# Transposes by DMA, a new order of TensorE's work, and a new division of the exponentials in a two-layer attention and gMLP kernel

## Chip, cores and metric

One core of a Trainium2 chip. The metric is the device time of one execution in microseconds (us). The record marks a run as slow when it is over 1.5% above the fastest of the same kernel. Each kernel's ratio is taken against runs of the kernel before on the same chip in the same rounds. Differences between two experiments are differences of medians, in part from other rounds and chips; the kernel before had medians of 1791.0 to 1793.1 us in all of them.

## The reference

Two layers, each an attention (32 query heads of 16, one key/value head) and a gated MLP with a spatial matrix `w_sp` of 2048 x 2048. S = 2048, D = 512.

```python
x = x + A(layernorm(x)); x = x + B(layernorm(x))      # twice, the same weights

def A(x):                                             # H = 32, Dh = 16
    q = (x @ wq).reshape(B, S, H, Dh).transpose(0, 2, 1, 3); k = x @ wk; v = x @ wv
    p = softmax(einsum('bhqd,bkd->bhqk', q, k) * Dh ** -0.5)
    return einsum('bhqk,bkd->bhqd', p, v).transpose(0, 2, 1, 3).reshape(B, S, H * Dh) @ wo

def B(x):
    z = gelu(x @ w_in); z1 = z[..., :896]; z2 = layernorm(z[..., 896:])
    g = einsum('ts,bsf->btf', w_sp, z2) + b_sp[None, :, None]
    return (z1 * g) @ w_out
```

The cost sits in the exponentials: 2 x 32 x 2048 x 2048 of them, in 4096 score blocks of 128 x 512 (in the kernel before ScalarE is busy with its part of them for 1474.0 of 1791.3 us).

## The kernel before

The program is scheduled in Python at build time: every operation is a task with a modelled cost, an event loop picks what each engine does next, and the order of each engine's instructions is then fixed.

```python
SHARE = 0.24; POOL_MAX = 4500; ACT_LOW = 1500; PV_MAX = 2      # (cut)
PASSES = ((0, 8), (8, 12), (12, 14), (14, 16))   # row tiles of each spatial pass
TERMS = ((0, 0.324...), (43, 0.253...), (85, 0.200...))        # three ramps: offset, weight

def do_exp(...):            # ScalarE: one or two score blocks at a time, PSUM -> slots of Pb
    e.activation(self.Pb[...], self.ps32[...], ACTF.Exp, scale=ESCALE)

def dve_block(...):         # or: three ramps in the bits of bf16 numbers
    # the first by VectorE from the score bank in PSUM (now and then another one too)
    e.tensor_scalar(self.Pi[:, sl[v].i, :], self.ps32[:, bank.i, :], EBIAS + lo, lo, op0=ALU.add, op1=ALU.max)
    # the others by GpSimd from the first one's slot in SBUF
    e.tensor_scalar(self.Pi[:, sl[v].i, :], self.Pi[:, sl[0].i, :], lo, 1.0, op0=ALU.add, op1=ALU.mult)

def step_pe(self):          # TensorE: scores, then value matmuls, then anything that is ready
    ...

def wsp_build(self):        # w_sp: 16 loads of 512 KB, 256 transposes on TensorE, copies, stores to HBM
    ...
```

The program's names in the profile: `ps_all` is the tile in PSUM that takes TensorE's results, in banks that must come free again; `Pb` is the tile in SBUF that holds the exponentials, in slots (`Pi` is the same tile read as int16). A block that goes to ScalarE takes one slot of `Pb` and one value matmul; an approximated block takes three of each.

The softmax here doesn't subtract the row's maximum and nothing guards it: scores larger than these inputs give would overflow.

## Time and profile before

| | before |
|---|---|
| time (median of 4) | 1792.14 us (1789.02 to 1794.14) |
| ScalarE busy / idle | 1579.6 / 211.7 us of a 1791.3 us span |
| exponentials' blocks on ScalarE / approximated | 3115 / 981 |

The prediction shows the totals, the slices, five stretches and the main groups. A group's line reads: line of the kernel, engine, operation, tile written <- tiles read, shapes, count | busy us, mean ns of one | idle us before it, and who ended that. A line of waits reads: who <- for whom: us in total, times, longest us. Two more readings matter later: the chain that ended last (the page's part 4, shares of the span by engine), and GpSimd's ramp by itself (shortest, median and longest in ns). The chain of the kernel before:

```profile
ACT 47%; PE 34%; POOL 8%; DVE 5%; issue 4%; DMA 1%; SPq 1%; DVEq 0%; ACTq 0%
```

Then the ramps that GpSimd makes, by line:

```profile
L1256 POOL TENSOR_SCALAR Pb<-Pb x1929: 619/620/742, 41.5 to 1719.4; 128x512 int16<-128x512 int16 x193
```

GpSimd's ramp takes 620 ns nearly always: only 7 of the 1929 take over 630. ScalarE leads the chain with 47%.

### The profile page before, as it was taken

The page shows a single profiled execution, that of the slowest core. Times are in us where ns is not written, and L with a number is a line of the kernel's source. Part 1 is how long each engine was busy: PE and PEld are TensorE (multiplying, and loading weights), DVE is VectorE, ACT ScalarE, POOL GpSimd, SP SyncE. Part 2 cuts the span into 40 slices and gives each one's busy share as a digit, 9 for nine tenths or more (in the row PEclk, how much of TensorE's full clock was granted, in tenths as well). Part 3 has the DMA queues.
Part 4 walks back from the last instruction along what each step waited for, and adds up shares of the span by engine and source line. Part 5 has one row for each costly group of instructions (what it writes and reads, how often), then busy time and mean ns, then how long its engine had stood idle before and what let it go on. Part 6 is the DMA issues. An engine that isn't in the chain of part 4 may idle for free.

```text
span 1791.3 us, 37444 instructions
## 1 busy us (share of the span) xinstructions
PE 1598.1 (89%) x14507; PEld 552.8 (31%) x14638; DVE 1116.0 (62%) x1894; ACT 1579.6 (88%) x2240; POOL 1341.0 (75%) x2262
## 2 busy tenths in 40 slices
PE   3999988888999999998999888887899999999998
PEld 2433322222322223233654222322232222233245
DVE  4777654455655575776876645555475566657766
ACT  2999999999899999997547999999999999999950
POOL 3788878788888887886346888788887888878830
PEclk9999999899999999999999999999999999999999
DMA  6015600000000000000000000000000000000001
GB/s 198 10 43 133 168 14 1 2 1 1 1 28 28 28 1 28 7 13 13 25 31 13 1 1 1 1 1 1 1 1 1 28 27 28 2 30 7 13 25 48
DMA packets 61662, 45.04 MB, mean 25 GB/s; under 512 B 35504, under 2 KB 58928, under 8 KB 61488
## 3 DMA queue, kind: packets, MB, share of 16 engines
q1 hardware_dynamic: 61488, 42.64, 8.2%
q8 instruction: 119, 1.95, 0.5%
q14 instruction: 55, 0.45, 0.1%
HBM read 32.15 MB, written 10.49 MB: 24 GB/s over the span
## 4 chain that ended last, share of the span: by engine, by line
ACT 47%; PE 34%; POOL 8%; DVE 5%; issue 4%; DMA 1%; SPq 1%; DVEq 0%; ACTq 0%
ACT Pb L1295 46%; PE ps_all L1167 8%; PE ps_all L1347 8%; POOL Pb L1256 6%; PE ps_all L997 5%; PE ps_all L897 3%; PE ps_all L939 3%; DVE Pb L1241 2%; PE ps_all L1051 2%; PE ps_all L703 1%; PE ps_all L1029 1%; ACT L1482 1%; POOL xn L568 1%; SPq L479 1%; PE ps_all L1027 1%
## 5 line engine op out<-in xcount | busy, mean ns | idle before, releaser
L1295 ACT ACTIVATE Pb<-ps_all 128x1024 bf16<-128x1024 f32 (+1 forms) x2053 | 1474.0, 961 | 48.5 <-PE ps_all L1167 40.2
L1256 POOL TENSOR_SCALAR Pb<-Pb 128x512 int16<-128x512 int16 x1929 | 1196.3, 620 | 277.0 <-DVE Pb L1241 135.3
L1241 DVE TENSOR_SCALAR Pb<-ps_all 128x512 int16<-128x512 f32 x1014 | 693.7, 689 | 523.8 <-PE ps_all L1167 501.4
L1167 PE MATMUL ps_all<-Q,kT 32*128 32x512 bf16 x4096 | 608.8, 389 | 116.5 <-ACT Pb L1295 86.9
L1347 PE MATMUL ps_all<-Pb,V 128*32 128x512 bf16 x6058 | 538.0, 390 | 10.3 <-POOL Pb L1256 3.1
L1167 PEld LDWEIGHTS ps_all<-Q,kT 32*128 32x128 bf16 x4096 | 155.7, 91 | 680.0 <-ACT Pb L1295 466.7
L997 PE MATMUL ps_all<-wstr,z 128*128 128x512 bf16 x695 | 206.0, 382 | 19.2 <-issue 8.8
L1347 PEld LDWEIGHTS ps_all<-Pb,V 128*32 128x32 bf16 x6058 | 125.4, 95 | 233.8 <-issue 81.1
L1005 DVE TENSOR_TENSOR gp<-ps_all,gp 128x512 f16<-128x512 f32 x112 | 74.6, 683 | 14.1 <-PE ps_all L997 13.6
L997 PEld LDWEIGHTS ps_all<-wstr,z 128*128 128x128 bf16 x784 | 50.8, 97 | 96.3 <-issue 51.8
L553 POOL TENSOR_SCALAR ln_rs<-ln_mv 128x1 f32<-128x1 f32 x64 | 14.1, 224 | 81.7 <-DVE ln_mv L559 79.3
L1051 PE MATMUL ps_all<-w_out,z 128*128 128x512 bf16 x205 | 54.9, 379 | 1.7 <-issue 0.8
L755 DVE CAST oT<-ps_all 128x512 bf16<-128x512 f32 x64 | 43.6, 686 | 15.9 <-PE ps_all L1347 15.8
L597 ACT ACTIVATE z<-ps_all 128x512 bf16<-128x512 bf16 x11 | 6.6, 597 | 52.8 <-PE ps_all L585 52.7
L910 DVE BATCH_NORM_STATS2 st<-z 128x6 f32<-128x448 bf16 x64 | 36.5, 609 | 24.1 <-ACT z L902 23.5
L897 PE MATMUL ps_all<-w_in,xnT 128*128 128x448 bf16 x256 | 50.8, 353 | 0.4 <-ACT Pb L1295 0.4
L939 PE MATMUL ps_all<-xnT,w_in 128*128 128x512 bf16 (+2 forms) x330 | 50.7, 307 | 0.3
L953 ACT ACTIVATE z<-ps_all 128x512 bf16<-128x512 f32 (+2 forms) x58 | 31.0, 581 | 21.0 <-PE ps_all L939 21.0
L1083 PE MATMUL ps_all<-ident,gp 128*128 128x128 bf16 x256 | 25.5, 231 | 24.4 <-DMA gp<-in_B_w_sp_dram 22.9
L1037 DVE TENSOR_TENSOR z<-ps_all,z 128x512 bf16<-128x512 f32 x64 | 38.3, 618 | 14.3 <-PE ps_all L1029 13.9
L1005 DVE TENSOR_TENSOR gp<-ps_all,bspc 128x512 f16<-128x512 f32 x56 | 38.4, 685 | 13.3 <-PE ps_all L997 12.1
L1027 PE MATMUL ps_all<-gp,ident 128*128 128x128 f16 x224 | 42.1, 224 | 4.6 <-DMA wstr<-wspt_scratch 2.7
(71 smaller groups left out, 944.6 us busy)
## 6 DMA issues: line engine op xcount, KB each, us to landing
wstr<-wspt_scratch SPq DMA_DIRECT2D x24, 512.0 KB, 4.1
gp<-in_B_w_sp_dram SPq DMA_DIRECT2D x16, 512.0 KB, 3.9
wspt_scratch<-gp SPq DMA_DIRECT2D x16, 512.0 KB, 4.8
wstr<-wspt_scratch SPq DMA_DIRECT2D x16, 256.0 KB, 2.7
out_dram<-X SPq DMA_DIRECT2D x16, 128.0 KB, 1.7
w_in<-in_B_w_in_dram SPq DMA_DIRECT2D x1, 1792.0 KB, 11.8
X<-in_A_x_dram SPq DMA_DIRECT2D x3, 512.0 KB, 6.9
bspc<-in_B_b_sp_dram SPq DMA_DIRECT2D x8, 128.0 KB, 4.7
```

Source lines behind the costliest of these rows:

```text
L755: ev = Task("dve", c_ps(512), lambda e, u=u, k=k: e.tensor_copy(self.oT[:, k, :], self.ps32[:, u.bank.i, :]), [self.oT_use[k]], 0.2, tag=" ...
L897: ins = e.matmul(self.ps32[:, b, 0:448], self.xnT2[:, buf, kd, o:o + P], self.w_in[:, kd, FH + h * 448:FH + (h + 1) * 448], start=(kd == 0 ...
L939: ins = e.matmul(self.ps32[:, b, i * nq:(i + 1) * nq], self.w_in[:, kd, f * P:(f + 1) * P], self.xnT2[:, buf, kd, 0:nq], start=(kd == 0), ...
L997: ins = e.matmul(self.ps32[:, b, :], self.z2[:, (s0 + i) % 8, f * P:(f + 1) * P], self.wstr[:, sl[i // 4][1], i % 4, :], start=(i == 0), s ...
L1005: return Task("dve", c_ps(512), lambda e: e.tensor_tensor(self.gp[:, tc, f, :], self.ps32[:, bank(), :], src, ALU.add), dps, 6.5, tag="gp")
L1027: e.matmul(out, self.ident16[:], self.gp[:, tc, f, o:o + P], start=True, stop=False)
L1051: ins = e.matmul(self.ps32[:, b, :], self.z1[:, tc, f, o:o + P], self.w_out[:, f, :], start=(f == 0), stop=(f == NF - 1))
L1167: ins = e.matmul(self.ps32[:, jb[i].i, :], self.kT[32 * j:32 * j + 32, u.half, kt * P:(kt + 1) * P], q, tile_position=(32 * j, 0), start=T ...
L1241: return lambda e: e.tensor_scalar(self.Pi[:, sl[v].i, :], self.ps32[:, bank.i, :], EBIAS + lo, lo, op0=ALU.add, op1=ALU.max)
L1256: return e.tensor_scalar(self.Pi[:, sl[v].i, :], self.Pi[:, sl[0].i, :], float(TERMS[v][0]), 1.0, op0=ALU.add, op1=ALU.mult)
L1295: return e.activation(self.Pb[:, s0:s0 + n, :], self.ps32[:, b0:b0 + n, :], ACTF.Exp, scale=ESCALE)
L1347: ins = e.matmul(self.ps32[32 * j:32 * j + 32, u.bank.i, :], self.V[:, var, kt, :], self.Pb[:, sl.i, :], tile_position=(0, 32 * j), start= ...
```

## The change

It is meant to free TensorE (transposes by DMA, less waiting in its order) and to use that room for more approximated blocks. It has five parts: transposes by DMA (with w_sp held back 25 us at the start), split spatial passes, an order of TensorE's work that must end before the next banks come free, a larger share, and a new way to make second and third ramps. The core of the diff:

```diff
-PASSES = ((0, 8), (8, 12), (12, 14), (14, 16))
-PORT = ("S", "xn", "z2n")          # VectorE tasks that the model makes wait for GpSimd
+PASSES = ((0, 4), (4, 8), (8, 12), (12, 14), (14, 16))
+PORT = ("xn", "z2n")
-    SHARE = 0.24
+    WSP_FROM = 25000
+    SHARE = 0.27
+    SHARE_HI = 0.30
-    ACT_LOW = 1500
-    POOL_MAX = 4500
+    ACT_LOW = 900
+    POOL_MAX = 2500
 # layer norms (all but the first two tiles and the last chunk), attention output, w_sp
+        return self.s.add(Task("sp", cost, lambda e: e.dma_start(dst, src, transpose=True), ...))
-    def wsp_build(self):   # (all of it)
 # (cut) step_pe
+        room = self.pack_due() + self.SLACK - s.t
+        k = s.pick("pe", lambda k: self.pe_cost(k) <= room + ...)
 # dve_block: second and third ramp
+            def fp(e, v=v, lo=lo):
+                return e.tensor_scalar(self.Pi[:, sl[v].i, :], self.Pi[:, sl[0].i, :], lo, 1.0, op0=ALU.add, op1=ALU.mult)
+            def fd(e, v=v, lo=lo):
+                src = self.Pi[:, sl[0].i, :]
+                return e.scalar_tensor_tensor(self.Pi[:, sl[v].i, :], src, lo, src, op0=ALU.add, op1=ALU.max)
+            self.either({"pool": (c_pool(512), fp), "dve": (c_ps(512), fd)}, [a], 3, ...)
```

More of the change, by code (lines that the diff above doesn't have):

```diff
@@ L376 @@
     SCORE_CAP = 6
+    WSP_FROM = 25000
     NPS = 24
+    NWS = 16
+    TA_PE = 2
+    GP_PRIO = 0.95
+    SP_PRIO = 3.5
     NROT = (2, 2)
-    SHARE = 0.24
+    SHARE = 0.27
+    SHARE_HI = 0.30
+    PE_LINE = 4000
     WARM = 0.6
     FILL_MIN = 2
-    ACT_LOW = 1500
-    POOL_MAX = 4500
+    ACT_LOW = 900
+    POOL_MAX = 2500
     DVE_MAX = 1500
@@ L386 @@
     PV_MIN = 3
-    PV_MAX = 2
-    PV_IDLE = 4
-    ACT_ONE = 9
+    PV_MAX = 3
+    PV_EFF = 0.7
+    PV_LEAST = 4
+    SLACK = 200
+    SLACK_HI = 200
+    MISC_T = 1500
+    ACT_ONE = 4
     ACT_MAX = 2
@@ L441, in alloc @@
         self.gp = self.sb([P, 4, NF, 512], FP16, "gp")
-        self.gp_flat = self.gp[:].bitcast(BF16).rearrange("p a f c -> p (a f c)")
-        self.wstr = self.sb([P, 4, 4, 512], BF16, "wstr")
+        self.wstr = self.sb([P, self.NWS, 512], BF16, "wstr")
         self.bspc = self.sb([P, 512], BF16, "bspc")
@@ L464, in alloc @@
         self.Pi = self.Pb[:].bitcast(I16)
-        self.wspT_d = nc.dram_tensor("wspt_scratch", [NT, P, S], BF16)
-        self.wspT_v = self.wspT_d.ap().rearrange("st p t -> p st t")
     def dve(self, cost, fn, deps=(), prio=5, tag="", **kw):
@@ L476, in either, with dma, cost, dma_t @@
         return self.s.add(Task(None, None, None, deps, prio, alts=alts, tag=tag, **kw))
-    def dma(self, dst, src, nbytes, deps=(), prio=5, tag="dma"):
-        return self.s.add(Task("sp", (60, 2000 + nbytes / 150.0), lambda e: e.dma_start(dst, src), deps, prio, tag=tag))
+    def dma(self, dst, src, nbytes, deps=(), prio=5, tag="dma", gate=None):
+        def cost():
+            done = max(self.s.t, self.dma_free) + nbytes / 280.0
+            self.dma_free = done
+            return 480, max(0.0, done - self.s.t) + 1500
+        return self.s.add(Task("sp", cost, lambda e: e.dma_start(dst, src), deps, prio, tag=tag, gate=gate))
+    def dma_t(self, dst, src, nbytes, deps=(), prio=5, tag="dmat", gate=None):
+        def cost():
+            done = max(self.s.t, self.dma_free) + nbytes / 200.0
+            self.dma_free = done
+            return 480, max(0.0, done - self.s.t) + 2000
+        return self.s.add(Task("sp", cost, lambda e: e.dma_start(dst, src, transpose=True), deps, prio, tag=tag, gate=gate))
     def attn_on(self):
@@ L575, in ln, with transp_dma, transp @@
         return d, k
-    def transp(self, tiles, xns, dst, prio, tag, extra=(), act_ok=True):
+    def transp_dma(self, xns, dsts, prio, tag, extra=()):
+        outs = []
+        for (tk, k), dst in zip(xns, dsts):
+            d = self.dma_t(dst, self.xn[:, k, :], 131072, [tk] + list(extra), prio - 0.5, tag)
+            self.xn_use[k] = d
+            outs.append(d)
+        return outs
+    def transp(self, tiles, xns, dst, prio, tag, extra=()):
         pieces = []
@@ L587, in fn @@
                 return ins
-            pieces.append((fn, c_mm(4, 128), [tk, self.t_ident]))
+            pieces.append((fn, c_mm(4, 128), [x[0] for x in xns] + [self.t_ident] if i == 0 else []))
         n = len(tiles)
@@ L606, in setup @@
         self.after = s.after
+        self.dma_free = 0.0
         self.xn_n = 0
@@ L727, in attn_inputs @@
             xs = [self.ln(t, xdeps[t], pr)]
-            dst = self.xnT(t)[:, None, :, :]
-            ev = self.transp([t], xs, dst, pr, "TA", extra=self.xnT_war[t])
+            if t < self.TA_PE:
+                ev = self.transp([t], xs, self.xnT(t)[:, None, :, :], pr, "TA", extra=self.xnT_war[t])
+            else:
+                ev = self.transp_dma(xs, [self.xnT(t)], pr, "TA", extra=self.xnT_war[t])[0]
             made, kout, vout = self.keys(t, ev, war, pr)
@@ L833, in fn @@
                     return ins
-                pieces.append((fn, c_mm(4, 128), norms[t] + [self.onT_use[x % 4] for x in pair if i == 0]))
+                pieces.append((fn, c_mm(4, 128), [y for x in pair for y in norms[x] + [self.onT_use[x % 4]]] if i == 0 else []))
             n = len(pair)
@@ L841, in mk @@
                 return Task("dve", c_2x(n * 512), fn, [lastp] + [self.onT_use[t % 4] for t in pair], 0.5, tag="onT")
-            made, outs = self.job(0.5, pieces, [mk], "TW")
-            for t, m in zip(pair, made):
-                self.on_use[t % 4] = m
+            if last:
+                made, outs = self.job(0.5, pieces, [mk], "TW")
+                for t, m in zip(pair, made):
+                    self.on_use[t % 4] = m
+                onT = {t: outs[0] for t in pair}
+            else:
+                onT = {}
+                for t in pair:
+                    onT[t] = self.dma_t(self.onT[:, :, t % 4, :], self.o_norm[:, t % 4, :], 131072,
+                                        norms[t] + [self.onT_use[t % 4]], 0.5, "TW")
+                    self.on_use[t % 4] = onT[t]
             for t in pair:
@@ L854, in mkx @@
                                 [lastp, self.Xv[t]], 0.6, tag="xadd")
-                made, ox = self.job(0.6, [(lambda e, b, wf=wf: wf(e, b, 0, 2), c_mm(2, 512), [outs[0], self.ldo]),
+                made, ox = self.job(0.6, [(lambda e, b, wf=wf: wf(e, b, 0, 2), c_mm(2, 512), [onT[t], self.ldo]),
                                           (lambda e, b, wf=wf: wf(e, b, 2, 4), c_mm(2, 512), [])], [mkx], "WO")
@@ L867, in attn_out @@
             o = q0 - base + a * P
-            dst = self.xnT2[:, buf, :, o:o + n * P].rearrange("p kd (t c) -> p t kd c", t=n)
-            evs.append(self.transp(pair, xs, dst, 0.8, "TB", extra=self.x2_use[buf]))
+            if last:
+                dst = self.xnT2[:, buf, :, o:o + n * P].rearrange("p kd (t c) -> p t kd c", t=n)
+                evs.append(self.transp(pair, xs, dst, 0.8, "TB", extra=self.x2_use[buf]))
+            else:
+                dsts = [self.xnT2[:, buf, :, o + i * P:o + (i + 1) * P] for i in range(n)]
+                evs += self.transp_dma(xs, dsts, 0.8, "TB", extra=self.x2_use[buf])
         for t in tl:
@@ L967, in slab @@
         n = s1 - s0
-        k = self.ws_n % 4
-        self.ws_n += 1
-        ld = self.dma(self.wstr[:, k, 0:n, :], self.wspT_v[:, s0:s1, tc * 512:(tc + 1) * 512], n * 512 * 256,
-                      list(self.wsp_done) + self.ws_use[k], prio=2, tag="ldw")
-        self.ws_use[k] = []
-        return ld, k
+        if self.ws_n % n:
+            self.ws_n += n - self.ws_n % n
+        k = self.ws_n % self.NWS
+        self.ws_n += n
+        war = [x for i in range(k, k + n) for x in self.ws_use[i]]
+        dst = self.wstr[:, k:k + n, :]
+        src = self.B_w_sp[tc * 512:(tc + 1) * 512, s0 * P:s1 * P]
+        ld = self.dma_t(dst, src, n * 131072, war, prio=2, tag="ldw", gate=lambda: self.s.t > self.WSP_FROM)
+        for i in range(k, k + n):
+            self.ws_use[i] = []
+        return ld, k, n
     def spatial(self, B, pi, final):
@@ L997, in gf @@
                             ins = e.matmul(self.ps32[:, b, :], self.z2[:, (s0 + i) % 8, f * P:(f + 1) * P],
-                                           self.wstr[:, sl[i // 4][1], i % 4, :], start=(i == 0), stop=(i == n - 1))
+                                           self.wstr[:, sl[i // 4][1] + i % 4, :], start=(i == 0), stop=(i == n - 1))
                         return ins
-                    pcs = [(lambda e, b, gf=gf, a=a: gf(e, b, a, a + 2), c_mm(2, 512), zd + lds + (self.gp_free if pi == 0 else []) if a == 0 else []) for a in range(0, n, 2)]
+                    pcs = [(lambda e, b, gf=gf, a=a: gf(e, b, a, min(a + 4, n)), c_mm(min(4, n - a), 512), zd + lds + (self.gp_free if pi == 0 else []) if a == 0 else []) for a in range(0, n, 4)]
                     def mk(lp, bank, f=f, tc=tc):
@@ L1005, in mk @@
                         return Task("dve", c_ps(512), lambda e: e.tensor_tensor(
-                            self.gp[:, tc, f, :], self.ps32[:, bank(), :], src, ALU.add), dps, 6.5, tag="gp")
-                    made, outs = self.job(7 - pi, pcs, [mk], "SP%d" % pi)
+                            self.gp[:, tc, f, :], self.ps32[:, bank(), :], src, ALU.add), dps, 1.05, tag="gp")
+                    made, outs = self.job(self.SP_PRIO + 0.1 * pi, pcs, [mk], "SP%d" % pi)
                     B.gpw[(tc, f)] = outs[0]
@@ L1013, in spatial @@
                     B.all += made
-            for _, k in sl:
-                self.ws_use[k] = self.ws_use[k] + use
+            for _, k, m in sl:
+                for i in range(k, k + m):
+                    self.ws_use[i] = self.ws_use[i] + use
         return xdeps
@@ L1029, in gf @@
                         ins = e.matmul(out, self.z2[:, (s0 + i) % 8, f * P:(f + 1) * P],
-                                       self.wstr[:, sl[i // 4][1], i % 4, o:o + P], start=False, stop=(i == n - 1))
+                                       self.wstr[:, sl[i // 4][1] + i % 4, o:o + P], start=False, stop=(i == n - 1))
                 return ins
@@ L1063, in last_pass @@
         return ox[0]
-    def wsp_build(self):
-        stage = [self.gp_flat[:, i * 2048:(i + 1) * 2048] for i in range(2)]
-        tile = [self.gp_flat[:, 4096 + i * 2048:4096 + (i + 1) * 2048] for i in range(2)]
-        st_use = [[], []]
-        tl_use = [[], []]
-        self.wsp_done = []
-        allw = []
-        for tt in range(NT):
-            k = tt % 2
-            ld = self.dma(stage[k], self.B_w_sp[tt * P:(tt + 1) * P, :], 524288, st_use[k], prio=5, tag="ldsp")
-            st_use[k] = []
-            evs = []
-            for hf in range(2):
-                def pf(e, b, lo, k=k, hf=hf):
-                    ins = None
-                    for i in range(lo, lo + 4):
-                        c = (hf * 8 + i) * P
-                        ins = e.transpose(self.ps16[:, b, i * P:(i + 1) * P], stage[k][:, c:c + P], self.ident[:])
-                    return ins
-                def mk(lp, bank, k=k, hf=hf):
-                    return Task("dve", c_2x(1024), lambda e: e.tensor_copy(
-                        tile[k][:, hf * 1024:(hf + 1) * 1024], self.ps16[:, bank(), :]), [lp] + tl_use[k], 7, tag="wspT")
-                made, outs = self.job(8, [(lambda e, b, pf=pf: pf(e, b, 0), c_mm(4, 128), [ld, self.t_ident]),
-                                          (lambda e, b, pf=pf: pf(e, b, 4), c_mm(4, 128), [])], [mk], "WT")
-                st_use[k].append(made[-1])
-                evs += outs
-            w = self.dma(self.wspT_v[:, :, tt * P:(tt + 1) * P], tile[k].rearrange("p (s c) -> p s c", c=P), 524288, evs, prio=4, tag="stsp")
-            tl_use[k] = [w]
-            self.wsp_done.append(w)
-            allw += st_use[k] + [w]
-        self.gp_free = allw
     def pack_ready(self):
@@ L1123, in backlog, with pe_line @@
     def backlog(self, eng):
-        return max(0.0, self.s.free[eng] - self.s.t) + sum(k.cost[0] for _, _, k in self.s.arm[eng] if k.start is None)
+        return max(0.0, self.s.free[eng] - self.s.t) + sum(
+            (k.alts[eng][0] if k.alts else k.cost)[0] for _, _, k in self.s.arm[eng] if k.start is None)
+    def pe_line(self):
+        return sum(k.cost[0] for _, _, k in self.s.arm["pe"] if k.start is None)
     def dve_backlog(self):
@@ L1135, in issue_pack @@
         k = len(blks)
-        self.credit = min(self.credit + k * self.SHARE, 2.5)
+        self.credit = min(self.credit + k * (self.SHARE if self.pe_line() > self.PE_LINE else self.SHARE_HI), 2.5)
         nd = min(2, k - 1, int(self.credit))
@@ L1212, in dve_block @@
     def dve_block(self, pk, u, kt, j, bank, n):
-        sl = []
         T = len(TERMS)
-        own = 1
-        while own < T and self.backlog("pool") + 700 * (T - own) > self.POOL_MAX and self.dve_backlog() + 600 * own < self.DVE_MAX:
-            own += 1
-        left = [own]
-        def read(task):
-            left[0] -= 1
-            if left[0] == 0:
-                self.free_bank(bank, task)
-        def hook(task):
-            bs = self.lone_slots(T)
-            self.pslots.take(bs[:1], task, 1 + T - own)
-            self.pslots.take(bs[1:], task)
-            sl.extend(bs)
-            self.need[n] -= T
-            def go():
-                read(task)
+        sl = [None] * T
@@ L1236, in go, with slot, h0 @@
+        def slot(v, task, refs=1):
+            b = self.lone_slots(1)
+            self.pslots.take(b, task, refs)
+            sl[v] = b[0]
+            self.need[n] -= 1
+        def h0(task):
+            slot(0, task, T)
+            def go():
+                self.free_bank(bank, task)
                 u.av[j].append((task.done, task, sl[0], 1, kt))
             self.after.append(go)
-        def ramp(v):
+        lo0 = float(TERMS[0][0])
+        a = self.dve(c_ps(512), lambda e: e.tensor_scalar(self.Pi[:, sl[0].i, :], self.ps32[:, bank.i, :], EBIAS + lo0, lo0, op0=ALU.add,
+                                                          op1=ALU.max), [pk], 1.0, gate=lambda: self.slot_ok(n, 1), hook=h0, tag="A")
@@ L1240, in ramp, with hv @@
+        for v in range(1, T):
             lo = float(TERMS[v][0])
-            return lambda e: e.tensor_scalar(self.Pi[:, sl[v].i, :], self.ps32[:, bank.i, :], EBIAS + lo, lo, op0=ALU.add, op1=ALU.max)
-        a = self.dve(c_ps(512), ramp(0), [pk], 1.0, gate=lambda: self.slot_ok(n, T), hook=hook, tag="A")
-        for v in range(1, T):
-            def hs(task, v=v):
+            def hv(task, v=v):
+                slot(v, task)
                 def go():
-                    if v < own:
-                        read(task)
-                    else:
-                        self.pslots.give(sl[0], task)
+                    self.pslots.give(sl[0], task)
@@ L1250, in go @@
                     u.av[j].append((task.done, task, sl[v], 1 + v, kt))
                 self.after.append(go)
-            if v < own:
-                self.dve(c_ps(512), ramp(v), [pk], 1.1, gate=lambda: a.start is not None, hook=hs, tag="A2")
-            else:
-                def fs(e, v=v):
-                    return e.tensor_scalar(self.Pi[:, sl[v].i, :], self.Pi[:, sl[0].i, :], float(TERMS[v][0]), 1.0, op0=ALU.add,
-                                           op1=ALU.mult)
-                self.pool(c_pool(512), fs, [a], 3, hook=hs, tag="S")
+            def fp(e, v=v, lo=lo):
+                return e.tensor_scalar(self.Pi[:, sl[v].i, :], self.Pi[:, sl[0].i, :], lo, 1.0, op0=ALU.add, op1=ALU.mult)
@@ L1260, in pick_exp @@
+            def fd(e, v=v, lo=lo):
+                src = self.Pi[:, sl[0].i, :]
+                return e.scalar_tensor_tensor(self.Pi[:, sl[v].i, :], src, lo, src, op0=ALU.add, op1=ALU.max)
+            self.either({"pool": (c_pool(512), fp), "dve": (c_ps(512), fd)}, [a], 3, gate=lambda: self.slot_ok(n, 1), hook=hv, tag="S")
     def pick_exp(self):
@@ L1391, in step_pe @@
         if pv is not None:
-            least = 1 if s.pe_mode == "pv" else self.PV_MIN
-            if pv[3] >= 4 * least or self.pv_hurry(pv):
-                self.do_pv(*pv[:3])
-                return True
-        k = s.pick("pe")
+            r = self.pv_depth(pv, room)
+            if r:
+                self.do_pv(r, pv[1], pv[2])
+                return True
+        late = s.t - self.misc_t > self.MISC_T
+        k = s.pick("pe", lambda k: self.pe_cost(k) <= room + (self.SLACK_HI if k.prio < 2.5 or late else 0))
@@ L1397, in step_pe, with pe_cost, pv_depth @@
         if k is not None:
             s.commit(k)
-            return True
-        if pv is not None and (pv[3] >= 4 * self.PV_IDLE or sum(pv[1].left) == pv[3]):
-            self.do_pv(*pv[:3])
+            self.misc_t = s.t
             return True
         return self.keep_warm()
+    def pe_cost(self, k):
+        return k.cost[0] + (100 if k.mode != self.s.pe_mode else 0)
+    def pv_depth(self, pv, room):
+        _, u, ls, tot = pv
+        sw = 100 if self.s.pe_mode != "pv" else 0
+        most = min(pv[0], self.PV_MAX, int((room - sw) // 216))
+        hurry = self.pv_hurry(pv)
+        if hurry:
+            most = max(most, 1)
+        for r in range(most, 0, -1):
+            n = sum(min(len(x), r) for x in ls)
+            if hurry or n >= 4 * r * self.PV_EFF and (sw == 0 or n >= self.PV_LEAST):
+                return r
+        return 0
@@ new lines, in pack_due @@
+    def pack_due(self):
+        s = self.s
+        t = s.t
+        if not self.attn_on() or self.batch is not None:
+            return t + 1e5
+        A = self.attns[self.ai]
+        for (u, kt, j) in A.blocks[A.nxt:A.nxt + 1]:
+            ds = A.kdep[kt] + [A.qdep[x] for x in range(u.q0 // P, (u.q0 + u.nq) // P)]
+            if any(d.start is None for d in ds):
+                return t + 1e5
+        extra = self.score_cap() - self.score_held
+        known = sorted(max(t, b.free) for b in self.banks.items if not b.held)[:max(extra, 0)]
+        a = max(t, s.free["act"]) + 170
+        known += [a + 450 * (i + 1) for i in range(len(self.act_q))]
+        d = max(t, s.free["dve"]) + 130
+        known += [d + 603 * (i + 1) for i in range(sum(1 for _, _, k in s.arm["dve"] if k.start is None and k.tag == "A"))]
+        known.sort()
+        e2 = known[self.FILL_MIN - 1] if len(known) >= self.FILL_MIN else t + 600
+        e4 = known[3] if len(known) > 3 else t + 1e5
+        dry = max(t, s.free["act"]) + 450.0 * len(self.act_q) - self.ACT_LOW
+        w = min(e4, max(e2, dry))
+        if w > t:
+            s.event(w)
+        return w
@@ L1490, in step_dve @@
         k = s.pick("dve", lambda k: k.alts is None or "pool" not in k.alts)
-        if k is None:
+        if k is None and self.backlog("pool") > self.POOL_MAX:
             k = s.pick("dve")
@@ L1541, in build @@
         self.unit_n = 0
+        self.misc_t = 0.0
         self.last_table = None
@@ L1549, in build @@
         self.x2_use = [[], []]
-        self.ws_use = [[] for _ in range(4)]
+        self.ws_use = [[] for _ in range(self.NWS)]
         self.bs_use = []
+        self.gp_last = []
         self.xnT_war = {t: [] for t in range(NT)}
@@ L1558, in build @@
                 u.attn = A
-            if layer == 0:
-                self.wsp_build()
-            else:
-                self.gp_free = list(self.gp_last)
+            self.gp_free = list(self.gp_last)
             self.z1_war = []
```

## The prediction

> **What bounds the kernel now.** I read four views in turn: the page (engine totals, then the slices), the groups by line, busy time by stretch, and the waits.
>
> The totals alone leave TensorE and ScalarE tied:
>
> ```profile
> PE 1598.1 (89%) x14507; PEld 552.8 (31%) x14638; DVE 1116.0 (62%) x1894; ACT 1579.6 (88%) x2240; POOL 1341.0 (75%) x2262
> ACT  2999999999899999997547999999999999999950
> DMA  6015600000000000000000000000000000000001
> ```
>
> The second and third lines cut the span into 40 slices of 45 us: ScalarE is full except in the first slice, in four around the middle and in the last two, and the DMA engines are empty after slice 5. [...] The waits decide:
>
> ```profile
> PEld ps_all L1167 <- ACT Pb L1295: 466.7, 956, 1.8
> ACT Pb L1295 <- PE ps_all L1167: 40.2, 53, 3.7
> ```
>
> The weight loads of the score matmuls (L1167) wait 467 us for ScalarE's exponentials (L1295) to give a PSUM bank back; ScalarE waits 40 us for scores. So in the bulk ScalarE's exponentials set the pace. By stretch (us; PE, PEld, DVE, ACT, POOL, then TensorE clock, DMA share, GB/s):
>
> ```profile
> 0.00:26.00 26.00, 3.09 (x28) 2.83 (x29) 4.95 (x16) 1.84 (x2) 6.54 (x29) 1.00 0.83 274
> 275.00:450.00 175.00, 143.75 (x1397) 39.45 (x1392) 92.29 (x141) 171.87 (x237) 143.26 (x234) 0.95 0.01 1
> 450.00:840.00 390.00, 368.71 (x3047) 110.43 (x3091) 246.04 (x404) 376.91 (x536) 321.43 (x538) 1.00 0.05 16
> 840.00:880.00 40.00, 38.40 (x365) 22.49 (x368) 34.97 (x70) 13.15 (x20) 9.19 (x20) 1.00 0.11 34
> 1730.00:1791.30 61.30, 54.15 (x509) 36.32 (x515) 41.07 (x69) 5.53 (x9) 0.91 (x3) 0.97 0.15 48
> ```
>
> Three regimes follow. In the bulk (90 to 840 and 965 to 1700) ScalarE is 97 to 98% busy. Around 840 to 965 and at the end TensorE is full and ScalarE starves: the last spatial pass, w_out and the next layer's keys and queries. At the start nothing runs. ScalarE's idle time, 1791 - 1580 = 211 us, is 35 before 90 us, 70 in the middle, 67 after 1700, and about 39 spread over the rest.
>
> The work per engine comes from these groups:
>
> ```profile
> L1295 ACT ACTIVATE Pb<-ps_all 128x1024 bf16<-128x1024 f32 (+1 forms) x2053 | 1474.0, 961 | 48.5 <-PE ps_all L1167 40.2
> L1256 POOL TENSOR_SCALAR Pb<-Pb 128x512 int16<-128x512 int16 x1929 | 1196.3, 620 | 277.0 <-DVE Pb L1241 135.3
> L1241 DVE TENSOR_SCALAR Pb<-ps_all 128x512 int16<-128x512 f32 x1014 | 693.7, 689 | 523.8 <-PE ps_all L1167 501.4
> L1347 PE MATMUL ps_all<-Pb,V 128*32 128x512 bf16 x6058 | 538.0, 390 | 10.3 <-POOL Pb L1256 3.1
> ```
>
> There are 4096 score blocks of 128x512 (L1167's count). A block goes to ScalarE (one result) or to an approximation of three ramps: the first by VectorE from PSUM, the others by GpSimd (L1256) or now and then VectorE. With n approximated blocks and a extra VectorE ramps, n + a = 1014 and 2n - a = 1929: n = 981, a = 33, a share of 0.2395, the SHARE of 0.24. Then ScalarE has 3115 blocks, 0.473 us each (1474.0 / 3115), and the value matmuls number 3115 + 3 x 981 = 6058, which is L1347's count.
>
> [...] The trace has no transposing DMA; its plain 512 KB loads land in 3.9 to 4.1 us. [...]
>
> **The change, part by part.**
>
> *Share.* The real lever hides behind the headline: SHARE goes from 0.24 to 0.27 (TensorE's queue over 4 us) or 0.30. Nominally that is 1106 to 1229 approximated blocks. The gate on VectorE's backlog will hold some back, so I take 1140 (0.278). ScalarE then loses 159 blocks x 0.473 = 75 us. Rule ACT_ONE = 4 turns some pairs into singles; a block in a pair is somewhat cheaper, so +8 us. Eleven or so transposed tiles that ScalarE evacuated (L597, 7.8 us) go: -6. ScalarE's work: 1580 - 75 + 8 - 6 = 1507.
>
> *Transposes off TensorE.* w_sp: 256 matmuls, 25.5 us, and 32 copies of 21.7 us on VectorE. Layer norms (L585): all but 2 x 2 + 2 tiles, 232 of 256, 23 us. Attention output (L831): 120 of 128, 11.5 us; copies about 28 us. So TensorE -60, VectorE -50. In the bulk this lies beside ScalarE's work and is worth little by itself: it makes room for the extra value matmuls, 2 x 159 = 318 at 538.0 / 6058 = 0.089 us, +28. Only in the middle is a piece on the path: 14 tiles x 0.40 us (four transposes in the timeline of 885 us) = 6 us.
>
> *VectorE and GpSimd.* 2280 second and third ramps now go to GpSimd, and to VectorE when GpSimd's backlog passes 2.5 us. All on GpSimd would be 2280 x 0.62 + 145 of other work = 1559 us, too near the span; I estimate 1850 there (1292 us) and 430 on VectorE. VectorE: 1116 + 159 x 0.69 - 33 x 0.69 + 430 x 0.69 (priced as an ordinary 128x512 operation, an estimate) + 56 extra gp additions x 0.68 - 50 = 1488 us, 88% of the new span. That makes it the second most crowded engine.
>
> *Start.* Now TensorE stands behind the w_sp loads, in program order, until 22.71 us:
>
> ```profile
> 22.71 1.03 PE L1083 MATMUL ps_all<-ident,gp 128*128 128x128 bf16 x8 [22.71 <-DMA gp<-in_B_w_sp_dram]
> 31.16 5.13 ACT L1295 ACTIVATE Pb<-ps_all 128x512 bf16<-128x512 f32 x10 [0.40 <-PE ps_all L1167]
> ```
>
> With w_sp held back to 25 us and two tiles left to TensorE, the first exponentials can run near 12 us. They cover 2 key tiles x 2 units x 4 = 16 blocks, some 7 us; then the transposed tiles arrive behind w_in and w_out in the same queue, which land near 21 us (issue at 8.2 plus 12.8), so full speed returns about 25 to 27 us. Worth 12 us.
>
> *Spatial passes.* Pass (0,8) is split and may begin after chunk 2, in 275 to 450 where TensorE has room, and its priority rises. Now 62 of its 128x512 matmuls (L997) run after 840 and 68 after 1700, where TensorE sets the end: 130 x 0.22 (spacing in the timeline) = 28 us, of which I count 10. With the 6 us of transposes: -16.
>
> *TensorE's order.* Work must fit before the next banks come free. This attacks ScalarE's 40 us of waiting for scores, 27 of which lie in the TensorE-full middle; I give it nothing beyond holding the bulk's waits level at the higher pace, and charge +5 for new waits.
>
> Sum: 1791 - 75 + 8 - 6 - 12 - 16 + 5 = 1695 us.
>
> **Rivals.**
> 1. *VectorE or GpSimd becomes the bound.* For: 88% on VectorE, GpSimd already 82% in the bulk[...]. Against: VectorE now idles 501 us waiting for scores and can be used. If so the realised share stays near 0.25 and the time is 1740 to 1760.
> 2. *Transposing DMAs are slow or queue behind 512 KB slabs*, so layer-norm tiles arrive late for keys and MLP batches. For: one queue for all, 16 MB of w_sp transposed for two layers. Against: [...]urgent tiles stay on TensorE. If so, the middle and the start lose 10 to 40 us: 1705 to 1735.
> 3. *TensorE becomes the bulk's bound*: 368.71 of 390 already in 450 to 840. Against: PEld's waits say this is slack. If so, nothing but the transposes counts: about 1750.
> 4. *More than counted*: the split passes empty the middle and the tail, and the share reaches 0.29: 1655.
>
> **Range and chances.** The sum stands on 75 us of share, whose size (50 to 110) is the largest doubt; the stages add 15 to 45. Rivals 1 to 3 each have perhaps one chance in eight and mostly still end below 1755. Range 1655 to 1745. Faster by over 2% (below 1755): 0.91; within 2%: 0.07; slower: 0.02.
>
> **What would show it.** Right: about 2950 exponentials' blocks at 0.47 to 0.48 us, ScalarE still 88% or more busy and 96% in the bulk; some 6380 value matmuls; no L1083 group; the first exponential near 12 us; fewer 128x512 spatial matmuls in the middle and tail; GpSimd's ramp still 620 ns. Wrong: GpSimd's mean above 700 ns or VectorE above 93% (rival 1); keys waiting on a DMA in the middle, landings over 6 us (rival 2); ScalarE's waits for L1167 above 100 us (rival 3). A share below 0.26 would break the main term.

The sum: 1791 - 75 + 8 - 6 - 12 - 16 + 5 = 1695 us. Its +8 is an estimate. That a block in a pair is cheaper shows in the trace before: the activation of a pair took 1168 ns in the mean (x1062), 584 a block, that of a single block 740 (x991).

## The result, and the profile after

| | before | after |
|---|---|---|
| time (median of 4) | 1792.14 us | 1841.48 us (1840.56 to 1843.43) |
| ratio | | 1.0278 (95%: 1.026 to 1.0296), slower |

A ratio here is the mean time of one kernel's fast runs over that of the kernel before in the same rounds, so not quite the ratio of the medians quoted. I had said 1695.

The page of the changed kernel: engine totals, ScalarE by slices, and the chain:

```profile
PE 1594.4 (87%) x14034; PEld 548.0 (30%) x14178; DVE 1437.4 (78%) x2375; ACT 1525.7 (83%) x2115; POOL 1476.6 (80%) x2251
...
ACT  6988889998799979994447888899988999799950
...
PE 29%; POOL 29%; ACT 13%; DVE 12%; issue 7%; DMA 0%; POOLq 0%; DVEq 0%; ACTq 0%
```

ScalarE's work fell, from 1579.6 to 1525.7 us, and its idle time rose by 101 us, from 211.7 to 313.0. GpSimd's share of the chain went from 8% to 29%. Fifteen of ScalarE's slices read 8 or 7; before, nearly all slices of the bulk read 9. The same bulk stretches as in the prediction (PE, PEld, DVE, ACT, POOL):

```profile
275.00:450.00 175.00, 151.62 (x1366) 45.08 (x1381) 141.62 (x218) 166.37 (x228) 156.20 (x227) 0.98 0.09 19
450.00:840.00 390.00, 340.68 (x2874) 107.46 (x2906) 301.21 (x486) 355.27 (x509) 339.31 (x522) 0.98 0.07 15
```

From 450 to 840 us ScalarE is 91% busy (97% before), TensorE's busy time is down too, and GpSimd is at 87% (82% before). The groups:

```profile
L1310 ACT ACTIVATE Pb<-ps_all 128x512 bf16<-128x512 f32 (+1 forms) x1928 | 1419.6, 860 | 165.9 <-PE ps_all L1189 97.8
L1268 POOL TENSOR_SCALAR Pb<-Pb 128x512 int16<-128x512 int16 x1918 | 1316.4, 686 | 212.2 <-DVE Pb L1254 46.2
L1254 DVE TENSOR_SCALAR Pb<-ps_all 128x512 int16<-128x512 f32 x1151 | 769.6, 684 | 251.5 <-PE ps_all L1189 206.3
L1362 PE MATMUL ps_all<-Pb,V 128*32 128x512 bf16 x6398 | 648.9, 399 | 131.6 <-POOL Pb L1268 78.0
...
L1272 DVE SCALAR_TENSOR_TENSOR Pb<-Pb 128x512 int16<-128x512 int16 x384 | 303.0, 794 | 15.9 <-POOL Pb L1268 9.8
```

L1254's count gives n = 1151 approximated blocks (a share of 0.281), so 2302 further ramps: 1918 on GpSimd (L1268) and 384 on VectorE (L1272). GpSimd's mean rose from 620 to 686 ns. The distribution says more than the mean:

```profile
L1268 POOL TENSOR_SCALAR Pb<-Pb x1918: 617/617/1175, 16.0 to 1767.8; 128x512 int16<-128x512 int16 x192
```

The median has hardly moved (617 after 620); some are nearly twice as long. I matched all GpSimd ramps of this trace with what VectorE ran at the same time: 567 that overlap a `scalar_tensor_tensor` last 851 ns on average, the other 1351 last 617. That is 567 x (851 - 617) = 133 us more on GpSimd. One such meeting, in order of time:

```profile
107.93 0.62 POOL L1268 TENSOR_SCALAR Pb<-Pb 128x512 int16<-128x512 int16 x1
...
108.06 1.03 DVE L1272 SCALAR_TENSOR_TENSOR Pb<-Pb 128x512 int16<-128x512 int16 x1
```

VectorE's ramp starts at 108.06, while GpSimd's is running until 108.55, and ends at 109.09: 0.54 us after GpSimd's. Elsewhere the one that waits is GpSimd's (936 ns from 50.13, beside a VectorE ramp that ends at 50.59). Unhindered, VectorE's takes about 0.68 us (the 23 that meet none of GpSimd's ramps: 681 ns in the median). Most of the trace's meetings go the same way. In 335 VectorE's ramp began first, and GpSimd's ended 476 to 478 ns after it (tenth to ninetieth percentile). In 249 GpSimd's began first, and in 176 of these VectorE's ended 530 to 559 ns after it. So the second ends a nearly fixed time after the first, as if they took turns. VectorE's ramps pay too, 384 x (0.794 - 0.68) = 44 us.

The start went as planned:

```profile
13.31 6.35 ACT L1310 ACTIVATE Pb<-ps_all 128x512 bf16<-128x512 f32 x8 [2.08 <-PE ps_all L1189]
27.02 1.02 ACT L1310 ACTIVATE Pb<-ps_all 128x1024 bf16<-128x1024 f32 x1 [7.35 <-PE ps_all L1189]
```

In both traces I then read when the n-th score matmul starts: the changed kernel is 19 us ahead at n = 256, level at n = 1792, 15 us behind at 2048 (11 of them at the change of layer) and 47 behind at the last. So most of the loss is made steadily in the full stretches.

### The profile page after: what moved, and what is told of

It reads as the page before. It is cut to its first block, busy times and chain, and to the rows that moved or that the text cites. A ratio compares the mean times of both kernels' runs of the same rounds, so it can differ in the third digit from the quotient of the medians.

```text
span 1838.7 us, 37665 instructions
## 1 busy us (share of the span) xinstructions
PE 1594.4 (87%) x14034; PEld 548.0 (30%) x14178; DVE 1437.4 (78%) x2375; ACT 1525.7 (83%) x2115; POOL 1476.6 (80%) x2251
## 4 chain that ended last, share of the span: by engine, by line
PE 29%; POOL 29%; ACT 13%; DVE 12%; issue 7%; DMA 0%; POOLq 0%; DVEq 0%; ACTq 0%
POOL Pb L1268 26%; ACT Pb L1310 12%; PE ps_all L1362 10%; PE ps_all L1189 7%; DVE Pb L1254 5%; PE ps_all L1047 2%; PE ps_all L942 2%; PE ps_all L984 2%; PE ps_all L1102 2%; DVE gp L1055 2%; DVE Pb L1272 2%; PE ps_all L1080 1%; POOL xn L589 1%; POOL ln_rs L575 1%; ACT L1541 1%
## 5 line engine op out<-in xcount | busy, mean ns | idle before, releaser
L1310 ACT ACTIVATE Pb<-ps_all 128x512 bf16<-128x512 f32 (+1 forms) x1928 | 1419.6, 860 | 165.9 <-PE ps_all L1189 97.8
L1268 POOL TENSOR_SCALAR Pb<-Pb 128x512 int16<-128x512 int16 x1918 | 1316.4, 686 | 212.2 <-DVE Pb L1254 46.2
L1254 DVE TENSOR_SCALAR Pb<-ps_all 128x512 int16<-128x512 f32 x1151 | 769.6, 684 | 251.5 <-PE ps_all L1189 206.3
L1362 PE MATMUL ps_all<-Pb,V 128*32 128x512 bf16 x6398 | 648.9, 399 | 131.6 <-POOL Pb L1268 78.0
L1189 PE MATMUL ps_all<-Q,kT 32*128 32x512 bf16 x4096 | 571.7, 396 | 64.3 <-ACT Pb L1310 26.9
L1272 DVE SCALAR_TENSOR_TENSOR Pb<-Pb 128x512 int16<-128x512 int16 x384 | 303.0, 794 | 15.9 <-POOL Pb L1268 9.8
L1362 PEld LDWEIGHTS ps_all<-Pb,V 128*32 128x32 bf16 x6398 | 156.0, 94 | 476.4 <-POOL Pb L1268 165.3
L1047 PE MATMUL ps_all<-wstr,z 128*128 128x512 bf16 x689 | 182.2, 384 | 17.7 <-issue 9.6
L1055 DVE TENSOR_TENSOR gp<-ps_all,gp 128x512 f16<-128x512 f32 x168 | 112.1, 685 | 40.1 <-PE ps_all L1047 39.2
L1080 PE MATMUL ps_all<-wstr,z 128*128 128x128 bf16 x448 | 46.7, 230 | 0.0
```

The lines of the kernel that those rows point to most:

```text
L1047: ins = e.matmul(self.ps32[:, b, :], self.z2[:, (s0 + i) % 8, f * P:(f + 1) * P], self.wstr[:, sl[i // 4][1] + i % 4, :], start=(i == 0), ...
L1055: return Task("dve", c_ps(512), lambda e: e.tensor_tensor(self.gp[:, tc, f, :], self.ps32[:, bank(), :], src, ALU.add), dps, 1.05, tag="gp")
L1080: ins = e.matmul(out, self.z2[:, (s0 + i) % 8, f * P:(f + 1) * P], self.wstr[:, sl[i // 4][1] + i % 4, o:o + P], start=False, stop=(i == n ...
L1189: ins = e.matmul(self.ps32[:, jb[i].i, :], self.kT[32 * j:32 * j + 32, u.half, kt * P:(kt + 1) * P], q, tile_position=(32 * j, 0), start=T ...
L1254: a = self.dve(c_ps(512), lambda e: e.tensor_scalar(self.Pi[:, sl[0].i, :], self.ps32[:, bank.i, :], EBIAS + lo0, lo0, op0=ALU.add, op1=AL ...
L1268: return e.tensor_scalar(self.Pi[:, sl[v].i, :], self.Pi[:, sl[0].i, :], lo, 1.0, op0=ALU.add, op1=ALU.mult)
```

## The experiments

**Theory:** VectorE's `scalar_tensor_tensor`, with two SBUF inputs, and GpSimd's ramps shut each other out (851 against 617 ns above), and GpSimd, 87% busy in the bulk, then holds everything up. **Rivals:** the new TensorE order starves ScalarE; the transposing DMAs cost time; the number of ramps binds GpSimd whatever VectorE runs; VectorE's ramps are just long.

### One instruction replaced, the order kept

```diff
-                return e.scalar_tensor_tensor(self.Pi[:, sl[v].i, :], src, lo, src, op0=ALU.add, op1=ALU.max)
+                return e.tensor_scalar(self.Pi[:, sl[v].i, :], src, lo, 1.0, op0=ALU.add, op1=ALU.mult)
```

> The changed kernel with one instruction replaced: the 384 ramps that VectorE makes from an SBUF ramp are tensor_scalar (one SBUF input) in place of scalar_tensor_tensor (the same SBUF tile as both inputs). Same modelled costs, so the same order of instructions on every engine. Theory 'two SBUF inputs on VectorE and GpSimd's ramp shut each other out' (567 GpSimd ramps that overlap one mean 851 ns, the others 617): GpSimd's mean falls from 686 to under 645 ns, VectorE's ramp from 794 to 400-500 ns, and the time falls to 1740-1790 us. Rival 'the new TensorE order starves ScalarE': the means change, the time stays within 1% of 1841. Rival 'the sheer number of ramps binds GpSimd': some fall, to 1800-1825.

Measured: 1718.88 us (1718.41 to 1720.89), ratio 0.960 (0.9586 to 0.9615). Counts of all engines are unchanged; the time fell by some 122 us, further than I had expected (1740 to 1790). GpSimd's and VectorE's groups in this kernel:

```profile
L1268 POOL TENSOR_SCALAR Pb<-Pb 128x512 int16<-128x512 int16 x1918 | 1194.1, 623 | 225.6 <-DVE Pb L1254 61.3
...
L1272 DVE TENSOR_SCALAR Pb<-Pb 128x512 int16<-128x512 int16 x384 | 168.7, 444 | 8.2 <-PE ps_all L1362 3.7
```

GpSimd is at 623 ns. The instruction is the loss; but this one is also shorter (444 ns), so it doesn't say whether the second SBUF input or the length mattered. Nor are the two engines quite apart here: the 25 of VectorE's ramps that meet no GpSimd ramp take 284 ns in the median and others up to 750, and the 590 GpSimd ramps that meet one mean 633 ns. The meetings are shorter, not gone.

### As long as before, but with one SBUF input

```diff
-                return e.scalar_tensor_tensor(self.Pi[:, sl[v].i, :], src, lo, src, op0=ALU.add, op1=ALU.max)
+                return e.tensor_reduce(self.Pi[:, sl[v].i, :], src[:, :, None], op=ALU.max, axis=mybir.AxisListType.X)
```

The offset is missing on purpose. The output still passed the comparison, so the comparison doesn't see an error of that size.

> The changed kernel with the same 384 VectorE ramps replaced by tensor_reduce over an axis of one element: one SBUF input, but [...]as long an instruction (expected 620-690 ns). The offset of the ramp is left out, so the result is wrong on purpose; the order of instructions is the same. Theory 'it is the second SBUF input that shuts GpSimd out': GpSimd's ramps back to 617-625 ns, time 1720-1760 us. Rival 'it is only VectorE's length, 0.69 against 0.39 us, with knock-on waits': GpSimd's ramp stays long or, if short, the time stays above 1800.

Measured: 1718.59 us (1712.99 to 1719.74), ratio 0.9573 (0.9549 to 0.9598), just below the range. The two groups by line:

```profile
L1268 POOL TENSOR_SCALAR Pb<-Pb x1918: 617/619/789, 16.4 to 1641.0; 128x512 int16<-128x512 int16 x192
```

```profile
L1272 DVE TENSOR_REDUCE Pb<-Pb x384: 628/677/687, 23.8 to 1637.1; 128x512 int16<-128x512 int16 x192
```

VectorE's ramp is as long as an unhindered `scalar_tensor_tensor` (677 ns), always so, and GpSimd's isn't stretched by it: the 617 that overlap one mean 620 ns. The rival "length" falls. The trace after holds a control as well: 163 GpSimd ramps run beside the gp addition of VectorE, which has two inputs but one of them in PSUM (and beside no `scalar_tensor_tensor`), and mean 617 ns, none over 619.

### All ramps on GpSimd

```diff
-            self.either({"pool": (c_pool(512), fp), "dve": (c_ps(512), fd)}, [a], 3, ...)
+            self.pool(c_pool(512), fp, [a], 3, ...)
```

> The changed kernel with VectorE's alternative removed: every second and third ramp on GpSimd, share kept (so some 2300 ramps on GpSimd, 2300 x 0.617 + 150 = 1570 us). The order of instructions changes. Theory 'GpSimd at 686 ns binds': GpSimd back to 617 ns; GpSimd full, 1720-1790 us, still below the changed kernel. Rival 'VectorE's help, even slow, is worth having': above 1841.

Measured: 1926.57 us (1924.85 to 1927.8), ratio 1.0738. My expectation failed and its rival held. GpSimd's ramp was 620 ns, but there were 2320 of them. ScalarE waited 97.5 us for their slots and 101.3 us for value matmuls (36.1 and 22.8 in the changed kernel). So at this share VectorE's help is needed, and even the hindered help was worth some 85 us (1926.57 - 1841.48; the order of instructions differs too). GpSimd wasn't full: 1582 of 1926 us, 88 to 89% in the bulk. How it holds the others up at that load wasn't taken apart.

### The parts undone one by one

`e_oldshare` undoes share and ramps, `e_oldpe` the order of TensorE's work, `e_tr2` both (the diffs in words):

```diff
-    SHARE = 0.27 / SHARE_HI = 0.30 / POOL_MAX = 2500, new dve_block and step_dve     # e_oldshare, e_tr2
+    SHARE = SHARE_HI = 0.24 / POOL_MAX = 4500, dve_block and step_dve of before
-    new step_pe, PV_MAX = 3, ACT_LOW = 900, ACT_ONE = 4                              # e_oldpe, e_tr2
+    step_pe of before, PV_MAX = 2, ACT_LOW = 1500, ACT_ONE = 9
```

> The changed kernel with only the exponentials' division as before: share 0.24, the old ramp code (second and third ramp on GpSimd, VectorE's extra ramps from PSUM), GpSimd's limit 4500. Transposes by DMA, split passes and the new TensorE order stay. Theory 'ramps on VectorE and the share cost the time': below the kernel before, 1740-1780 us, GpSimd's ramp back at 620 ns. Rival 'TensorE order': still about 1820-1840. Rival 'transposing DMAs': still about 1820-1840.

Measured: 1746.5 us (1745.9 to 1749.97), ratio 0.9757; GpSimd's ramp 618 ns.

> The changed kernel with only the order of TensorE's work as before (old choice, ACT_LOW 1500, ACT_ONE 9, PV_MAX 2). Share, ramps and transposes stay as changed. Theory 'ramps': GpSimd's ramp still about 680 ns, time 1820-1860. Rival 'TensorE order': 1740-1790.

Measured: 1910.32 us (1904.19 to 1913.41), ratio 1.0663; GpSimd's ramp 683 ns. A miss to the far side: without the new order it is slower still.

> Both undone: the old division of the exponentials and the old TensorE order; what stays is the transposes by DMA, w_sp read transposed from HBM, and the split spatial passes with their new priorities. Theory 'the headline is sound, the ramps are the loss': 1750-1775 us, first exponential near 13 us. Rival 'transposing DMAs cost': 1790 or more.

Measured: 1784.96 us (1778.55 to 1796.35), ratio 0.9988 (0.9954 to 1.0022), not told from the kernel before and between my two guesses. So transposes by DMA with the split passes are neither a loss nor a gain that this shows. The start's gain (11 us, below) is inside this, and so is a cost: with the old order ScalarE waits 76.4 us for scores here, 40.2 in the kernel before; with the new one (`e_oldshare`) it is 44.2. Thus the rival "DMA" falls as a cause of the loss, and the rival "TensorE order" is the reverse of one: it is worth 38 us at the old share (1784.96 - 1746.5) and 69 beside the hindered ramps.

### The same parts, with the mended ramp

Each starts from `e_ts`: `e_ts_24` sets the share back, `e_ts_oldpe` the order, `e_ts_trpe` the transposes of layer norms and attention output (w_sp stays with the DMA). The diffs are shortened, and against `e_ts`.

```diff
+    SHARE = SHARE_HI = 0.24                  # e_ts_24
+    (step_pe of before and its constants)    # e_ts_oldpe
-    TA_PE = 2                                # e_ts_trpe
+    TA_PE = 16
-            if last:      # both places
+            if True:
```

> e_ts (changed kernel, tensor_scalar ramps) with the share back at 0.24. What the larger share is worth once ramps don't shut each other out. My prediction gave it 75 us of ScalarE's work and 67 net; e_oldshare (other ramp code, share 0.24) was 1746. Theory 'most of it is given back as waits': 1735-1750, so worth 15-30 us. Rival 'it is worth what was predicted': 1775-1790.

Measured: 1755.89 us (1753.13 to 1758.03), ratio 0.9796. The larger share is worth some 37 us by medians, 35 by the ratios (0.0196 of 1791), between my two guesses.

> e_ts with the old order of TensorE's work. Theory 'the new order is the largest gain, which I had put at nothing': 1755-1800, that is 40-80 us above e_ts (with the old share it was 1785 against 1746.5; with the slow ramps 1910 against 1841). Rival: within 10 us of e_ts.

Measured: 1774.11 us (1762.09 to 1779.17), ratio 0.9889. The order is worth some 55 us, with more spread between runs than elsewhere.

> e_ts with the transposes of layer norms and attention output back on TensorE and VectorE; w_sp stays transposed by DMA. Theory 'they lie beside other work': 1720-1740, a gain of 0.1 to 1.2% for the DMA. Rival 'TensorE is short of room at this pace': above 1745.

Measured: 1714.13 us (1712.78 to 1718.71), ratio 0.9569 (0.9547 to 0.959), below the range. Against 0.960 for `e_ts` (0.9586 to 0.9615), on another chip, the DMA transposes of these two kinds gain nothing, though TensorE's busy time rises from 1553.7 to 1585.1 us without them: that time lay beside other work.

### The start alone

The kernel before with its w_sp loads held back until 25 us of the scheduler's clock:

```diff
-            ld = self.dma(stage[k], self.B_w_sp[tt * P:(tt + 1) * P, :], 524288, st_use[k], prio=5, tag="ldsp")
+            ld = self.s.add(Task("sp", ..., st_use[k], 5, tag="ldsp", gate=lambda: self.s.t > 25000))
```

> The kernel before with one edit: the loads of w_sp wait for 25 us of the scheduler's clock, so TensorE doesn't stand behind them. All else as before. If the start is worth what the traces show (4095 score matmuls aside, 15 to 18 us ahead at the first 256 blocks): 1772-1782. Rival 'the start is given back by later waits, since w_sp's transposes then fall in the full stretch': within 5 us of 1791.

Measured: 1779.77 us (1777.57 to 1780.83), ratio 0.9932. That is 11 us for one gate.

### A version that beats both

The scheduler is told a shorter length for VectorE's ramp, then also that it waits for GpSimd. The length, 208 ns, is the scheduler's own figure for short operations and not a measured one: the shortest of `e_ts` took 228 ns, the median 390. The diff is against `e_ts`:

```diff
-            self.either({"pool": (c_pool(512), fp), "dve": (c_ps(512), fd)}, [a], 3, ...)
+            self.either({"pool": (c_pool(512), fp), "dve": (c_4x(512), fd)}, [a], 3, ...)    # e_ts4
-PORT = ("xn", "z2n")
+PORT = ("S", "xn", "z2n")                                                                 # e_ts4p also
```

> [...] The order changes. Expected to beat e_ts a little: 1700-1720 us; if the order alone already fits, no change (within 0.5%).

> e_ts4 with the scheduler also told that a VectorE ramp waits for GpSimd's running one, as it is told for the layer norm's tensor_scalar. Theory: the wait is real but short (GpSimd's ramps in e_ts: 92 of 1918 over 650 ns), so modelling a full exclusion moves ramps about: within 1% of e_ts4, 1695-1730 us.

Measured: `e_ts4` 1713.76 us (1712.85 to 1718.68), ratio 0.9562 (0.9534 to 0.9589); `e_ts4p` 1708.19 us (1706.92 to 1711.9), ratio 0.9525 (0.9503 to 0.9547). `e_ts4p` has the lowest time of all and is 4.7% below the kernel before; its interval lies below that of `e_ts` (0.9586 to 0.9615) and overlaps that of `e_ts4`. Its ramps on VectorE number 558 and GpSimd's mean is 624 ns.

## Why the prediction was wrong

**The step that failed is "VectorE and GpSimd"**, where 430 ramps on VectorE were "priced as an ordinary 128x512 operation". Each was charged 0.69 us. As `scalar_tensor_tensor` with two SBUF inputs, 384 of them came to 794 ns each, and they stretched GpSimd's by 133 us. I had written rival 1 for a bound on one of the two engines, and had named the sign to look for, a GpSimd mean above 700 ns (it was 686, since only 567 of 1918 were hit). But I charged nothing for it in the sum, let its chance be one in eight, and put its cost at 1740 to 1760. It turned 1719 into 1841. Rival 1's form was wrong too: the share didn't stay near 0.25, it came out at 0.281.

I had also written that the trace before can't show a GpSimd slowed beside VectorE. It does: the 7 GpSimd ramps of over 630 ns in it (679 to 742) all run beside the layer norm's `tensor_scalar` on VectorE, from SBUF to SBUF (L565); 13 others that meet it take 619 to 621. (Another reading there was narrow, without effect: "3.9 to 4.1 us" is for the w_sp loads; other 512 KB loads, at the start, took 5.0 to 7.8.)

The trace after and the pair `e_ts`, `e_red` show together: GpSimd's ramp takes 617 ns alone, 851 on average beside a `scalar_tensor_tensor`, 633 beside a `tensor_scalar`, 620 beside a `tensor_reduce` of 677 ns. The diff showed where to look: `fd` lists `src` twice, and it takes "S" out of the list of tasks that wait for GpSimd.

Why 122 us and not more or less isn't worked out from these lengths alone. In profiled spans, `e_ts` against the changed kernel has 27.3 us less ScalarE work (1525.7 to 1498.4) and 94.5 us less ScalarE idle. The waits name most of the idle part. First the changed kernel:

```profile
ACT Pb L1310 <- PE ps_all L1189: 97.8, 124, 7.3
...
ACT Pb L1310 <- POOL Pb L1268: 36.1, 49, 2.6
...
ACT Pb L1310 <- PE ps_all L1362: 22.8, 41, 2.3
```

Then `e_ts`, the same order of instructions:

```profile
ACT Pb L1310 <- PE ps_all L1189: 59.2, 47, 7.4
...
ACT Pb L1310 <- PE ps_all L1362: 7.0, 11, 2.1
...
ACT Pb L1310 <- POOL Pb L1268: 5.8, 10, 1.8
```

That is 156.7 against 72.0 us. I read it so (argued from these waits, not tried): ScalarE's exponentials wait for GpSimd mostly at second hand: a late ramp delays a value matmul that stands in TensorE's fixed order (TensorE waited 78.0 us for L1268 there, 8.3 in `e_ts`), and the scores behind it come late.

**The other terms**, against the runs:

| term | predicted | measured, and from which runs |
|---|---|---|
| number of blocks | 2956 on ScalarE | 2945 |
| share, with pairs | -67 | -37 (`e_ts_24` to `e_ts`) |
| start | -12 | -11 (`b_start`); the first exponential at 13.3 for "near 12" |
| ScalarE's transposed tiles | -6 | no run alone |
| layer-norm and output transposes in the middle | -6 of the -16 | 0 (`e_ts_trpe`) |
| spatial passes in the middle and tail | -10 of the -16 | not seen: 140 spatial weight loads from 836 to 965 and after 1717 before, 148 in the like stretches after |
| TensorE's order | +5 for new waits | -38 to -55 (`e_tr2` to `e_oldshare`, `e_ts_oldpe` to `e_ts`) |
| VectorE's ramps beside GpSimd's | 0 | +122 (after to `e_ts`) |

The share's mechanism was right and its size wrong: with the mended ramp ScalarE's work falls by 71.7 us (1570.1 in `e_ts_24` to 1498.4), close to the 75 foreseen, but half of it comes back as idle. The order of TensorE's work was the largest gain and I gave it none, because I read ScalarE's 40 us of waiting for scores as all there was to win. But the other parts raise these waits when the order is old: to 76.4 us in `e_tr2` and 99.9 in `e_ts_oldpe`, against 44.2 and 59.2 with the new order. That is 32 and 41 of the 38 and 55 us; the split of the order's gain between its rules wasn't tried. Without the ramps' term, the predicted 1695 stood beside 1719 measured, inside the range, but by errors that partly cancel.

The headline was read rightly as worth little in the bulk; rival 2 (late transposing DMAs) did not come about: in the changed kernel the engines' waits for transposed tiles add up to 6.4 us, and landings are 2.4 to 2.5 us in the median (3.3 for the layer norm's of the first 60 us), and 4.0 for a piece of w_sp.

**Open:** TensorE's granted clock fell to 0.967 (0.985 before, 0.991 in `e_ts`), with 0.78 from 1058 to 1104 us; how much that added to the loss wasn't told apart. The loss doesn't need it, though. From 92 to 230 us the clock is 0.98 in the changed kernel and in `e_ts`, in this order (PE, PEld, DVE, ACT, POOL), and ScalarE is busy 121 against 134 us:

```profile
92.00:230.00 138.00, 109.97 (x1063) 34.16 (x1066) 116.34 (x186) 120.82 (x168) 123.96 (x172) 0.98 0.03 7
...
92.00:230.00 138.00, 124.15 (x1176) 39.59 (x1175) 111.44 (x210) 133.81 (x191) 120.20 (x196) 0.98 0.04 9
```

The kernels with the old order also run at a lower clock (0.920 to 0.930 in `e_oldpe`, 0.958 to 0.967 in the changed kernel; 0.970 to 0.985 in `e_tr2`, 0.987 to 0.992 in `e_oldshare`), so part of the order's worth may lie there. No run has another VectorE operation with two SBUF inputs, or `scalar_tensor_tensor` with only one: that the second SBUF input is the reason, and nothing else about that operation, is read from `e_red` (620 ns) and the control with the gp addition (617 ns), and not shown by itself. The gain of the w_sp transposes alone wasn't run.

## What to carry to other kernels

Before an operation moves to VectorE beside a busy GpSimd, count its SBUF tensor inputs, one tile named twice as two: `scalar_tensor_tensor` with the same tile twice made GpSimd's ramp 851 ns on average in place of 617. `tensor_scalar`, with one, met GpSimd too, for a shorter time (633 ns); `tensor_reduce`, with one, left it at 620. Test it by swapping only that instruction and keeping the order, once for a shorter one and once for one of the same length. In a program whose order is fixed at build time, a conflict that the cost model doesn't know comes back as time (133 us of stretched GpSimd ramps stood beside 122 us of loss here), and a change of many parts should be timed part by part before its headline gets the credit or the blame.
